# An attention, gated-product and soft-mixture kernel: the gated rows turned by VectorE through DRAM in all batches but the last third of the last, and weight slots opened where the block products end

## The chip, the core and the metric

The kernel runs on one core of a Trainium2 chip. The metric is the device time of one execution in microseconds (us); it is compared as a median of several runs. Engines are named as the profile names them: PE (TensorE, matmuls; PEld its weight loads), DVE (VectorE), ACT (ScalarE), POOL (GpSimd), SP (SyncE, which here only issues transfers).

## What is computed

Four batches of 448 tokens. Attention with a sigmoid in the place of the softmax gives x (1792 x 768); a gated product makes g = (x w_a) * (x w_b), 1536 wide, and x = g w_out; a soft mixture of 8 experts with 32 slots works on that. The reference, cut:

```python
scores = scale * np.matmul(q, k.transpose(0, 1, 3, 2)) - np.log(S)      # S = 448, 12 heads of 64
x = np.matmul(1 / (1 + np.exp(-scores)), v)  # -> (4 * 448, 768)
x = ((x @ w_a) * (x @ w_b)) @ w_out          # 768 -> 1536 -> 768
logits = x @ phi                             # 32 slots
d = softmax(logits, axis=0)                  # over all 1792 tokens
slot_input = (d.T @ x).reshape(8, 4, 768)
for e in range(8):
    slot_out[e] = np.maximum(slot_input[e] @ w1[e], 0) @ w2[e]   # 768 -> 1024 -> 768
out = softmax(logits, axis=1) @ slot_out
```

## The kernel before

All matrices are float32. Weights and x are split into a high and a low part (h, l), so that one product is three matmuls in a fast format.

x is never multiplied by w_out for all tokens. Since d.T @ (g w_out) = (d.T @ g) w_out, the kernel needs G = d.T @ g (32 x 1536) only, and multiplies that by w_out once, at the end. The logits come from g and w_out phi, computed early. G needs g with tokens on partitions, while the products leave it with the 1536 columns on partitions, in 12 chunks (fc) of 128 x 448 per batch. `group(b, gi)` takes four chunks (gi = 0, 1, 2), adds their share of the logits (`project`, L581), and turns them in one of two ways. For gi of 0 and 1, DVE turns 32 x 32 blocks (L603), four SP transfers write them to the DRAM tensor gk32 in runs of 512 bytes (`store_gk`, L641), and two transfers read them back with tokens on partitions in runs of 2 KB (`reload_gk`, L646 and L647). For gi of 2, PE transposes 16 blocks of 128 x 128 (L624), and DVE and ACT copy the four banks out (L626). `LG(b)` makes the logits' exponentials and adds the batch's share of G (`dg`, L936: 48 matmuls, 96 in the trace).

The stages follow each other in one hand-written order per engine. (1) Attention of all batches, with the products of batch 0 (`ab(0)`, L660) in its second quarter. A background job meanwhile rewrites the weights: w_a and w_b to the DRAM tensor ab32, w_out to out32. (2) `unit(u)`, u = 0 to 11: the products of batches 1 and 2 together, as seven block products each (L843). (3) `ab(3)`: the products of batch 3, 72 steps of 6 matmuls. Step i belongs to chunk i // 6; each chunk uses 6 KB per partition of weights, two transfers of 384 KB (`load_w`, L542), numbered LAST + 0 to LAST + 23, that are cast by DVE (L550) and subtracted by POOL (L551). In its first 28 steps the last groups of batches 1 and 2, then LG(1) and LG(2), are mixed in. (4) `last_LG`: logits and G of batch 3. (5) The expert part: G times w_out (L1229), 24 blocks of w1 (1 MB each) in six products of four (L1249), 32 blocks of w2 (768 KB) in eight products of four (L1275), then the output (L1301, L1322, L1323).

The blocks of w_out, w1 and w2 form one queue. `pump()` issues the next one into the next free slot of 8 KB per partition (L1074 for w_out, L1085 for most of w1 and w2, L1080 and L1083 for halves of the last eight blocks of w2). `done(what)` gives a slot back when a product has used it, and pumps again. Slots come from pools that are opened when earlier buffers die: 11 of pool e1 at step 6 of ab(3), two after LG(1), three after LG(2), gkp0 when the last weights no longer use it, e10 after the last weight block, three of e2 when ab(3) is over, the fourth (e20) after G is finished. Before any slot comes back there are thus 22: 5 of w_out and 17 of w1. pump is called every third step of ab(3), from step 12 on.

All transfers but a few stand in SP's one queue, in program order. Each waits for the tiles that it writes to be free, for the data that it reads, and for the eighth transfer before it to have landed, so that at most eight are under way; what stands behind a waiting transfer waits too.

## Time and profile before

| | us |
|---|---|
| median of 3 runs (662.77 to 665.39) | 664.79 |
| the profiled execution | 664.73 |
| its span, first to last instruction | 662.8 |
| PE busy in it | 633.0 (96%) |
| DVE, ACT, POOL busy | 380.1, 296.6, 308.4 |
| HBM read and written | 126.36 MB, 27.17 MB |

The page gives busy times over the span and in 40 slices, the traffic, the costliest groups of instructions, and the chain of work that ended last: from the last instruction back, at each step, to what released it. Other views answer for a stretch: busy time and transfer rate of a window, instructions in order of time, waits, and transfers with their time from issue to landing. A matmul's end is modelled, so a PE that is busy all the time is not PE at its peak.

### The profile page before, as it was taken

The page shows a single profiled execution, that of the slowest core. Times are in us where ns is not written, and L with a number is a line of the kernel's source. Part 1 is how long each engine was busy: PE and PEld are TensorE (multiplying, and loading weights), DVE is VectorE, ACT ScalarE, POOL GpSimd, SP SyncE. Part 2 cuts the span into 40 slices and gives each one's busy share as a digit, 9 for nine tenths or more (in the row PEclk, how much of TensorE's full clock was granted, in tenths as well). Part 3 has the DMA queues.
Part 4 walks back from the last instruction along what each step waited for, and adds up shares of the span by engine and source line. Part 5 has one row for each costly group of instructions (what it writes and reads, how often), then busy time and mean ns, then how long its engine had stood idle before and what let it go on. Part 6 is the DMA issues. An engine that isn't in the chain of part 4 may idle for free.

```text
span 662.8 us, 10904 instructions
## 1 busy us (share of the span) xinstructions
PE 633.0 (96%) x4015; PEld 449.9 (68%) x4015; DVE 380.1 (57%) x557; ACT 296.6 (45%) x534; POOL 308.4 (47%) x236
## 2 busy tenths in 40 slices
PE   6999999999999999999999999999999998997685
PEld 4557777777776555489988989888879895442121
DVE  4765797788774879588777766744324322200013
ACT  4888889889774677754423322202010002110022
POOL 0233676777644248579976575543334441000000
PEclk9999999999999999999999999999999999998798
DMA  9998999989968676501213423242999999999998
GB/s 204 280 258 221 298 305 291 314 268 300 278 166 184 112 150 143 179 1 47 96 49 103 111 89 101 69 134 80 347 372 333 384 369 344 410 415 416 409 374 303
DMA packets 145396, 154.25 MB, mean 233 GB/s; under 512 B 74336, under 2 KB 121792, under 8 KB 142272
## 3 DMA queue, kind: packets, MB, share of 16 engines
q1 hardware_dynamic: 138768, 150.01, 72.5%
q10 hardware_dynamic: 6576, 3.56, 1.9%
q8 instruction: 32, 0.52, 0.3%
q14 instruction: 20, 0.16, 0.1%
HBM read 126.36 MB, written 27.17 MB: 232 GB/s over the span
## 4 chain that ended last, share of the span: by engine, by line
PE 83%; DMA 11%; ACT 2%; DVE 2%; issue 1%; ACTq 1%; SPq 0%; DVEq 0%
PE ab L660 28%; PE sc L843 16%; DMA e<-in_moe_w 9%; PE sc L243 8%; PE ab L843 8%; PE sc L273 5%; PE ab L279 3%; PE ms L195 2%; PE ms L936 2%; PE ms L581 1%; DMA gkp<-in_moe_w 1%; PE ms L480 1%; PE ms L493 1%; PE ab L243 1%; ACT a L249 1%; PE ab L286 1%
## 5 line engine op out<-in xcount | busy, mean ns | idle before, releaser
L454 POOL TENSOR_TENSOR w<-gk,cy 128x768 int32<-128x768 int32 x36 | 66.2, 1842 | 80.1 <-DVE gk L449 35.3
L249 ACT ACTIVATE a<-sc,sums 112x448 f32<-112x448 f32 (+1 forms) x147 | 83.1, 650 | 15.8 <-PE sc L243 15.7
L660 PE MATMUL ab<-t,wh 128*128 128x448 f32 x288 | 65.1, 371 | 0.0
L660 PEld LDWEIGHTS ab<-t,wh 128*128 128x128 f32 x288 | 53.4, 188 | 6.1 <-issue 1.3
L551 POOL TENSOR_TENSOR wl<-wr,wh 128x768 fp32r<-128x768 f32 x16 | 29.5, 1841 | 49.7 <-DVE wh L550 31.9
L551 POOL TENSOR_TENSOR wl<-w,wh 128x768 fp32r<-128x768 f32 x24 | 45.0, 1878 | 10.1 <-ACT wh L550 10.1
L667 ACT COPY misc<-ab 128x448 f32<-128x448 f32 x24 | 12.7, 531 | 82.1 <-PE ab L660 75.2
L1275 PE MATMUL ab<-e,gk 128*32 128x384 f32 x240 | 34.3, 560 | 9.5 <-DMA e<-in_moe_w 9.5
L670 DVE TENSOR_TENSOR misc<-misc,ab 128x448 f32<-128x448 f32 x24 | 14.8, 616 | 43.9 <-PE ab L660 43.9
L273 PE MATMUL sc<-a,vn 112*64 112x448 f32 x192 | 38.7, 545 | 0.2 <-ACT a L249 0.2
L243 PE MATMUL sc<-qh,kh 64*112 64x448 f32 (+1 forms) x147 | 34.9, 447 | 1.0 <-ACT qh L183 0.6
L723 ACT CAST wx<-T 128x384 fp32r<-128x384 f32 x21 | 10.8, 513 | 55.7 <-DVE T L745 39.1
L660 PE MATMUL ab<-xh,wh 128*128 128x448 f32 x144 | 34.9, 377 | 0.0
L660 PE MATMUL ab<-xl,wh 128*128 128x448 f32 x144 | 34.7, 376 | 0.0
L724 POOL TENSOR_TENSOR wx<-T,wx 128x384 fp32r<-128x384 f32 x23 | 24.6, 1070 | 21.1 <-ACT wx L723 18.0
L660 PE MATMUL ab<-xh,wl 128*128 128x448 f32 x144 | 34.3, 373 | 0.0
L660 PE MATMUL ab<-t,wl 128*128 128x448 f32 x144 | 34.3, 373 | 0.0
L724 POOL TENSOR_TENSOR wx<-wr,wx 128x384 fp32r<-128x384 f32 x29 | 32.4, 1117 | 3.7 <-ACT wx L723 3.6
L1322 DVE COPY o<-sc 128x384 f32<-128x384 f32 x10 | 5.4, 554 | 48.2 <-PE sc L1301 47.0
L447 DVE TENSOR_SCALAR mf<-gk 128x768 f32<-128x768 f32 x24 | 22.7, 947 | 17.2 <-ACT gk L430 17.2
L660 PEld LDWEIGHTS ab<-xl,wh 128*128 128x128 f32 x144 | 25.9, 188 | 9.4 <-issue 7.7
L1275 PEld LDWEIGHTS ab<-e,gk 128*32 128x32 f32 x240 | 9.8, 120 | 32.8 <-DMA e<-in_moe_w 20.7
(492 smaller groups left out, 1526.6 us busy)
## 6 DMA issues: line engine op xcount, KB each, us to landing
e<-in_moe_w SPq DMA_DIRECT2D x23, 1024.0 KB, 8.5
e<-in_moe_w SPq DMA_DIRECT2D x23, 768.0 KB, 15.1
wr<-ab SPq DMA_DIRECT2D x14, 768.0 KB, 4.4
ab<-w SPq DMA_DIRECT2D x24, 384.0 KB, 6.4
gk<-gk SPq DMA_DIRECT2D x24, 224.0 KB, 4.0
e<-in_moe_w SPq DMA_DIRECT2D x14, 384.0 KB, 8.8
wr_cv<-in_moe_w_a SPq DMA_DIRECT2D x6, 768.0 KB, 7.9
wr_all<-in_moe_w_b SPq DMA_DIRECT2D x6, 768.0 KB, 6.8
```

What stands on the lines that cost most here:

```text
L243: pe.matmul(sc[h], kx[r, cs], qx[r], start=(i == 0), stop=(i == 2))
L249: act.activation(a, sc, AF.Sigmoid, bias=nlog[:n], scale=1.0 / math.sqrt(D))
L273: pe.matmul(pv[64 * h:64 * h + 64], qkv_t["v", g][:, h, c, :], a_t.pop((g, h, c)), start=(c == 0), stop=(c == C - 1))
L279: pe.matmul(pv[64 * h:64 * h + 64], qkv_t["v", g][:, h, c], a_t.pop((g, h, c)), start=(c == 0), stop=False)
L447: dve.tensor_scalar(mf, m, LOW, HIGH, op0=ALU.max, op1=ALU.min)
L454: pool.tensor_tensor(thirds(w), m.bitcast(I32), thirds(cy_t.pop(x)), op=ALU.add)
L551: pool.tensor_tensor(wl, t, wh.bitcast(F32), op=ALU.subtract)
L660: pe.matmul(t, w[:, kk * 128:(kk + 1) * 128], xt[b * NP + kk][xi], start=(s == 0 and kk == 0), stop=(s == 2 and kk == KD - 1))
L670: dve.tensor_tensor(g, g, t, op=ALU.mult)
L724: pool.tensor_tensor(w[:, 1], t, w[:, 0].bitcast(F32), op=ALU.subtract)
L843: pe.matmul(t, w[:, wi, k * 128:(k + 1) * 128], xs[ORDER[m], k][xi], start=(s == 0 and k == 0), stop=(s == 2 and k == 2))
L1275: pe.matmul(sps[h][32 * j:32 * j + 32], hT[:, 2 * x + i, 2 * j + g], ring[order2[n + j]][0][:, i, c0:c0 + w], start=(g == 0 and x == 0 and ...
```

## The change

- Group 2 of batches 0, 1 and 2 goes the way of groups 0 and 1: DVE turns it, SP stores it, and it is read back. Only group 2 of batch 3 keeps PE's transposes.
- For batches 0 to 2 (TURNED) gk32 gets another layout (t outside n), so that 112 partitions read 8 KB of adjacent bytes each in one transfer, in the place of two transfers with runs of 2 KB. The token order of `weights` and of the exponentials (written with strides) follows from that, and `dg` uses 112 rows in all four parts. Batch 3 keeps the old layout.
- w_out is read as five pieces of a row of 9216 values: four of 8 KB per partition, one of 4 KB; before, three with runs of 2 KB and two with runs of 1 KB. Pieces cut one chunk in two, so that the product has 25 matmuls, not 24.
- Tiles swap places. Of the block products' g, units 0, 1, 6 and 7 use pool xb and units 2, 3, 8 and 9 use gT_all. r0, r1, r2, x3t and the weights' wr move from pool cp to a new pool hp. So xb and cp die with the last unit, and e1 (14 tiles) opens there with eight slots and three tiles each for the reloads of batches 1 and 2; hp dies at step 6, and a pool f1 (3 tiles) takes its place. pump is called from step 0. Batch 3's first chunks wait for the group that still holds their tile (held_by). The groups of batch 1 are now all filed ahead of those of batch 2.
- The number of slots before one comes back: eight of e1, f12, three after LG(1), f11 and three after LG(2), gkp0, f10, four of e2, which is 22.

The diff, cut:

```diff
-NE1, NE2 = 17, 4
+NE1, NF1, NE2 = 14, 3, 4
-    gk32 = drp.tile([B, 2, S, 512], F32, name="gk32")
+    gk32 = [[drp.tile([32, S // 32, 512] if b in TURNED else [S // 32, 32, 512], F32, name=f"gk32_{b}{gi}")
+             for gi in range(3 if b in TURNED else 2)] for b in range(B)]
...
+    def turns(b, gi):
+        return gi < 2 or b in TURNED
...
-        if gi < 2:
+        if turns(b, gi):
             turned = gk[:, :4 * S].rearrange("p (n f) -> p n f", f=128)
...
     def reload_gk(b, gi, t):
+        if b in TURNED:
+            sp.dma_start(out=t[:T], in_=gk32[b][gi].rearrange("t n f -> (t n f)").rearrange("(p x) -> p x", p=T))
+            gtok[b, gi] = t.rearrange("p (c n) -> p c n", c=C)
+            return
...
+    held_by = (None, KF + 8, 2 * KF + 9, 2 * KF + 8, KF + 9)
...
-                            while n - 5 in live or (n % KF == 4 and b and run["lg"] < b - 1):
+                            while n - 5 in live or (n % KF == 4 and b and run["lg"] < b - 1) or (b == B - 1 and held_by[n % 5] in live):
                                 fill_step()
...
         if k < 4:
-            return gT_all[k + 1]
+            return pools["xb"].tile([128, S], F32, tag=f"g{k}", name=f"g{k}")
         if k < 8:
-            return pools["xb"].tile([128, S], F32, tag=f"g{k}", name=f"g{k}")
+            return gT_all[k - 3]
...
-        if b == B - 3:
-            open_slots(run["e1"], [2, 3])
-        elif b == B - 2:
+        if b == B - 2:
             run.pop("lsd2")
-            open_slots(run["e1"], [1, 4, 5])
+            open_slots(run["f1"], [1])
+        if b:
+            open_slots(run["e1"], gtiles[b])
...
+        store_gk(0, 2, turned_0[2])
...
-            i = what[1]
-            if i < 3:
-                t = t.rearrange("p (a n) -> p a n", a=4)
-                src = out32[:, 4 * i:4 * i + 4, :512]
-            else:
-                t = t[:, :6 * 256].rearrange("p (a n) -> p a n", a=6)
-                src = out32[:, 6 * (i - 3):6 * (i - 3) + 6, 512:]
-            sp.dma_start(out=t, in_=src)
+            src = out32.rearrange("p k n -> p (k n)")[:, 2048 * what[1]:min(2048 * what[1] + 2048, KF * DM)]
+            sp.dma_start(out=t[:, :src.shape[1]], in_=src)
...
+    cp_ctx.close()
+    xb_ctx.close()
+    e1 = run["e1"] = ctx.enter_context(tc.tile_pool(name="e1", bufs=1, side="right"))
+    back = [(b, gi) for b in gtiles for gi in range(3)]
...
+    reload_next()
+    reload_next()
+    open_slots(e1, range(6, NE1))
     for i, frac in enumerate(ab(B - 1)):
...
-            open_slots(e1, range(6, NE1))
+            open_slots(f1, [2])
...
-        if i >= 12 and i % 3 == 0:
+        if back and 6 <= i:
+            reload_next()
+        if i % 3 == 0:
             pump()
```

DVE's order from the last unit (L836, L845) into batch 3 before, with L550 the cast of a weight block, L670 the product of a and b:

```order
L836 TENSOR_TENSOR x3t<-x3t,gk_94 128x448
L585 TENSOR_TENSOR misc<-misc,sc 128x448
L626 COPY gk_93<-ms 128x512
L550 CAST wh_4983<-wr 128x768
L626 COPY gk_93<-sc 128x512
L585 TENSOR_TENSOR misc<-misc,ms 128x448
L670 TENSOR_TENSOR misc<-misc,ab 128x448
L626 COPY gk_93<-sc 128x512
L550 CAST wh_5037<-wr 128x768
L626 COPY gk_93<-ms 128x512
```

The same place in the changed kernel (L609 is the turning, L553 the cast, L680 the product, L588 the sum of logits):

```order
L845 TENSOR_TENSOR x3t<-x3t,gk_94 128x448
L588 TENSOR_TENSOR misc<-misc,sc 128x448
L609 STREAM_TRANSPOSE gk_93<-misc 128x14x32 x2
L609 STREAM_TRANSPOSE gk_93<-r_4764 128x14x32
L609 STREAM_TRANSPOSE gk_93<-x3t 128x14x32
L553 CAST wh_4973<-wr 128x768
L588 TENSOR_TENSOR misc<-misc,ms 128x448
L609 STREAM_TRANSPOSE gk_93<-misc 128x14x32 x2
L680 TENSOR_TENSOR misc<-misc,ab 128x448
L609 STREAM_TRANSPOSE gk_93<-r_4811 128x14x32
L609 STREAM_TRANSPOSE gk_93<-r_4794 128x14x32
L553 CAST wh_5013<-wr 128x768
```

Eight turnings stand where four copies of PSUM banks stood, and the two casts keep their places behind them.

SP's queue from the end of the block products before; ab is ab32 (weights), out is out32 (w_out), gk_102 is gk32:

```order
L542 DMA gk_94<-ab_99 128x768 x2
L542 DMA wr<-ab_99 128x768 x2
L646 DMA e_5063<-gk_102 128x3x512
L647 DMA e_5063<-gk_102 64x512
...
L542 DMA gk_94<-ab_99 128x768
L1074 DMA e_5141<-out_100 128x4x512
L542 DMA gk_94<-ab_99 128x768
L1074 DMA e_5174<-out_100 128x4x512
```

The same place in the changed kernel (L545 is load_w, L645 the stores, L649 a reload, L1083 w_out; gk_12_107 is batch 1, group 2):

```order
L545 DMA gk_94<-ab_99 128x768 x2
L649 DMA e_4937<-gk_10_105 112x2048
L649 DMA e_4939<-gk_11_106 112x2048
L1083 DMA e_4948<-out_100 128x2048
L645 DMA gk_12_107<-gk_93 448x1x128 x4
L1083 DMA e_4988<-out_100 128x2048
L645 DMA gk_22_110<-gk_93 448x1x128 x4
L545 DMA wr<-ab_99 128x768 x2
L649 DMA e_5036<-gk_12_107 112x2048
L1083 DMA e_5038<-out_100 128x2048
...
L1083 DMA e_5076<-out_100 128x2048
L545 DMA gk_94<-ab_99 128x768
```

Two reloads and two pieces of w_out moved ahead of the weights LAST + 6 and LAST + 7 (wr), eight stores came in between, and four reloads and two pieces of w_out stand ahead of LAST + 8 (the last row).

SP's queue over the last third of ab(3) in the changed kernel; L1094 is a block of w1, L654 and L655 the reloads of batch 3, the last row but one is e20:

```order
L1094 DMA e_5554<-in_moe_w 128x2048
L1094 DMA gkp_5580<-in_moe_w 128x2048
L545 DMA wr<-ab_99 128x768 x4
L654 DMA gk_93<-gk_30_111 128x3x512
L655 DMA gk_93<-gk_30_111 64x512
L654 DMA gk_93<-gk_31_112 128x3x512
L655 DMA gk_93<-gk_31_112 64x512
L1094 DMA f_5741<-in_moe_w 128x2048
L1094 DMA e_5789<-in_moe_w 128x2048
L1094 DMA e_5791<-in_moe_w 128x2048
L1094 DMA e_5793<-in_moe_w 128x2048
L1094 DMA e_5899<-in_moe_w 128x2048
```

Before, blocks of w1 stood between the last four weight loads (wr); now they are all ahead of them, and gkp, the last of them, is pumped at step 48.

## Rows read from the trace of the kernel before

**Rows 1.** The page, busy tenths in 40 slices of the span:

```profile
PE   6999999999999999999999999999999998997685
PEclk9999999999999999999999999999999999998798
DMA  9998999989968676501213423242999999999998
```

**Rows 2.** The chain that ended last, 545 us on: start, length, engine and line:

```profile
550.42 0.88 PE ms L581 x6
...
556.36 3.48 PE ab L936 x96
...
561.64 4.08 PE sc L1229 x48
...
569.54 3.69 PE sc L1249 x32
573.24 0.22 SPq L1085
573.54 10.98 DMA e<-in_moe_w
...
630.16 8.36 DMA gkp<-in_moe_w
638.56 1.49 PE ab L1275 x10
```

**Rows 3.** Windows: length, busy time per engine, PE clock, DMA share, GB/s:

```profile
440.00:460.00 20.00, 20.00 (x119) 16.39 (x118) 9.73 (x17) 2.88 (x5) 5.58 (x4) 1.00 0.09 23
460.00:500.00 40.00, 40.00 (x361) 32.20 (x361) 14.20 (x32) 4.94 (x13) 13.74 (x8) 1.00 1.02 353
573.00:647.00 74.00, 61.03 (x453) 21.44 (x449) 5.77 (x11) 6.22 (x13) 0.00 (x0) 0.93 1.03 404
```

**Rows 4.** SP's instructions in order of time, 455 us on: start, length, line:

```profile
458.48 0.80 SPq L542 DMA_DIRECT2D wr<-ab  x2
...
547.27 12.95 SPq L1085 DMA_DIRECT2D e<-in_moe_w  x5
561.38 0.59 SPq L1218 DMA_DIRECT2D misc<-clog  x1
562.77 24.02 SPq L1085 DMA_DIRECT2D e<-in_moe_w  x16
```

**Rows 5.** Line 1085, the three blocks issued when ab(3) ends, and their landing:

```profile
L1085 SPq DMA_DIRECT2D e<-in_moe_w x3: 346/431/432, 550.4 to 551.3; - x3
...
DMA to landing us min/median/max: 6.0/8.0/10.0
```

**Rows 6.** The chain by line over 441 to 476 us, and its piece at chunk 4:

```profile
by line: PE ab L660 64.4%; PE ms L936 9.8%; PE sc L843 6.4%; PE ms L624 5.9%; PE sc L624 5.0%; PE sc L581 2.5%; PE ms L581 2.5%; PE ms L881 2.1%; PE sc L925 1.0%; PE sc L919 0.9%
...
485.01 1.41 PE ab L660 x6
```

**Rows 7.** Line 603, turnings on DVE: shortest, median, longest in ns, first and last start:

```profile
L603 DVE STREAM_TRANSPOSE gk<-r x3: 630/633/636, 396.5 to 416.2; 128x448 f32<-128x448 f32 x3
```

**Rows 8.** The chain that ended last, 210 to 220 us:

```profile
211.88 1.45 DVE kl L184
...
217.43 1.02 PE ms L624 x8
...
219.25 0.59 PE ms L624 x4
```

**Rows 9.** SP in order of time, one k load (four transfers) of attention:

```profile
254.94 2.09 SPq L153 DMA_DIRECT2D kn<-in_k  x4
```

**Rows 10.** DVE in order of time, the first use of that load:

```profile
265.52 0.63 DVE L191 STREAM_TRANSPOSE kn<-kn 128x448 f32<-128x448 f32 x1
```

**Rows 11.** Line 641, SP's stores of batches 1 and 2:

```profile
L641 SPq DMA_DIRECT2D gk<-gk x16: 303/650/1256, 355.2 to 430.1; - x16
...
DMA to landing us min/median/max: 2.7/4.0/5.5
```

**Rows 12.** Line 646, the 2 KB part of the reloads of batches 1 and 2:

```profile
L646 SPq DMA_DIRECT2D e<-gk x4: 587/638/1581, 459.3 to 463.9; - x4
...
DMA to landing us min/median/max: 6.8/8.4/11.0
```

**Rows 13.** Line 542, the weights LAST + 6 and LAST + 7:

```profile
L542 SPq DMA_DIRECT2D wr<-ab x2: 320/372/424, 458.5 to 458.9; - x2
...
DMA to landing us min/median/max: 4.0/4.3/4.6
```

**Rows 14.** Line 542, the weights LAST + 5:

```profile
L542 SPq DMA_DIRECT2D gk<-ab x1: 333/333/333, 444.6 to 444.6; - x1
...
DMA to landing us min/median/max: 3.0/3.0/3.0
```

**Rows 15.** Line 550, casts of weight blocks on DVE:

```profile
L550 DVE CAST wh<-wr x6: 518/552/560, 449.3 to 498.5; 128x768 fp32r<-128x768 f32 x6
```

More of the change, by code (lines that the diff above doesn't have):

```diff
@@ L46, in body @@
     stat = ctx.enter_context(tc.tile_pool(name="stat", bufs=2, side="left"))
-    ps_ctx, ab_ctx, x0_ctx, cv_ctx, at_ctx, cp_ctx, xb_ctx = (ctx.enter_context(ExitStack()) for _ in range(7))
+    ps_ctx, ab_ctx, x0_ctx, cv_ctx, at_ctx, hp_ctx, cp_ctx, xb_ctx = (ctx.enter_context(ExitStack()) for _ in range(8))
     lgp = ctx.enter_context(tc.tile_pool(name="lgp", bufs=1, side="left"))
@@ L300, in raw_x @@
         nm = f"r{kk}" if b == 2 else "x3t"
-        return pools["cp"].tile([128, S], F32, tag=nm, name=nm)
+        return pools["hp"].tile([128, S], F32, tag=nm, name=nm)
     def emit_x(g):
@@ L535, in body @@
     LAST = 2 * (NCH - KF)
+    gtiles = {1: (0, 1, 2), 2: (3, 4, 5)}
     def load_w(x):
@@ L604, in group @@
                 yield
-                if b < B - 1:
+                if b < B - 1 and gi < 2:
                     yield
@@ L618, in group @@
         gk = gk.rearrange("p (c n) -> p c n", c=C)
-        if gi == 2 and not b:
-            yield
         for c in range(C):
@@ L692, in ab @@
                         run.pop("wr")
-                        open_slots(run["e1"], [0])
+                        open_slots(run["f1"], [0])
                         pump()
@@ L864, in unit @@
         if u % 4 == 3:
+            fill.append(group(1, u // 4))
             fill.append(group(2, u // 4))
-            fill.append(group(1, u // 4))
     def col():
@@ L920, in tokens, with weights @@
         dve.tensor_copy(dst, t)
-    def weights(d, dst):
+    def weights(b, d, dst):
         t = ms((128, C, NS))
+        if b in TURNED:
+            for c in range(C):
+                pe.transpose(t[:T, c], d[:NS, c::C], ident[:NS, :NS])
+            dve.tensor_copy(dst[:T], t[:T])
+            return
         for c in range(C):
@@ L956, in rest_LG @@
     def rest_LG(b, dtok):
-        weights(run["lsd"][1], dtok)
+        weights(b, run["lsd"][1], dtok)
         for _ in range((3, 4, 1)[b]):
@@ L960, in rest_LG @@
         gp = ms((128, FF // 4))
-        for groups in ((0,), (1,), (2,)):
-            dg(b, dtok, gp, groups)
+        for gi in range(3):
+            dg(b, dtok, gp, gi)
         if b:
@@ L995, in last_LG @@
         dtok = wphi[:, 4:4 + C]
-        weights(run["lsd"][1], dtok)
+        weights(B - 1, run["lsd"][1], dtok)
         for _ in gr:
@@ L1000, in last_LG @@
         gp = ms((128, FF // 4))
-        for groups in ((0,), (1,), (2,)):
-            dg(B - 1, dtok, gp, groups)
+        for gi in range(3):
+            dg(B - 1, dtok, gp, gi)
         dve.scalar_tensor_tensor(acc, acc, run["al"], gp, op0=ALU.mult, op1=ALU.add)
@@ L1176, in body, with reload_next @@
     load_w(LAST + 5)
+    cp_ctx.close()
+    xb_ctx.close()
+    e1 = run["e1"] = ctx.enter_context(tc.tile_pool(name="e1", bufs=1, side="right"))
+    back = [(b, gi) for b in gtiles for gi in range(3)]
+    def reload_next():
+        b, gi = back.pop(0)
+        nm = f"e1{gtiles[b][gi]}"
+        reload_gk(b, gi, e1.tile([128, 2048], F32, tag=nm, name=nm))
+    reload_next()
+    reload_next()
+    open_slots(e1, range(6, NE1))
     for i, frac in enumerate(ab(B - 1)):
@@ L1183, in body @@
                 fill_step()
-            cp_ctx.close()
-            xb_ctx.close()
-            e1 = run["e1"] = ctx.enter_context(tc.tile_pool(name="e1", bufs=1, side="right"))
-            run["lsd2"] = e1.tile([128, 2048], F32, tag="e11", name="lsd2")
-            run["wr"] = e1.tile([128, 2048], F32, tag="e10", name="wr")
+            hp_ctx.close()
+            f1 = run["f1"] = ctx.enter_context(tc.tile_pool(name="f1", bufs=1, side="right"))
+            run["lsd2"] = f1.tile([128, 2048], F32, tag="f11", name="lsd2")
+            run["wr"] = f1.tile([128, 2048], F32, tag="f10", name="wr")
             load_w(LAST + 6)
             load_w(LAST + 7)
-            for x in range(4):
-                nm = f"e1{2 + x}"
-                reload_gk(1 + x // 2, x % 2, e1.tile([128, 2048], F32, tag=nm, name=nm))
-            open_slots(e1, range(6, NE1))
+            open_slots(f1, [2])
             fill.append(LG(1))
@@ L1223, in body @@
     for what in order0:
-        i = what[1]
-        h, n, f0 = (0, 4, 4 * i) if i < 3 else (1, 6, 6 * (i - 3))
-        for x in range(n):
-            fc = f0 + x
-            j = fc % 4
-            pe.matmul(sip[h][32 * j:32 * j + 32, :512 - 256 * h], GT[:, fc * NS:(fc + 1) * NS], ring[what][0][:, x],
-                      start=(fc < 4), stop=(fc >= 8))
+        lo, hi = 2048 * what[1], min(2048 * what[1] + 2048, KF * DM)
+        cuts = [c for fc in range(KF) for c in (fc * DM, fc * DM + 512) if lo < c < hi]
+        for a, z in zip([lo] + cuts, cuts + [hi]):
+            fc, n0 = divmod(a, DM)
+            h, j = n0 // 512, fc % 4
+            n0 -= 512 * h
+            pe.matmul(sip[h][32 * j:32 * j + 32, n0:n0 + z - a], GT[:, fc * NS:(fc + 1) * NS],
+                      ring[what][0][:, a - lo:z - lo], start=(fc < 4), stop=(fc >= 8))
         done(what)
```

36 lines of the change are left out of this document (19 added, 17 removed).

## The prediction

> **What bounds the kernel now.** I read the page's slices first, then the chain of waits, then the same stretch by windows and by SP's instructions in order of time.
>
> The slices [rows 1] show two regimes. PE is at nine tenths in every slice but the first up to the expert part, at a granted clock of nine tenths or more. The DMA line is low in the third quarter (the block products of batches 1 and 2), full again from about slice 28, and full to the end. The chain [rows 2] tells which of them ends last where both are high. Up to the product of G by w_out (L1229, at 561.64) it is PE pieces; behind the first w1 product (L1249, at 569.54) it is a row of transfers, the first of them issued at 573.24 and the last block (gkp) landing at 638.5, then the short output. So the kernel is bound by PE up to about 562 and by DMA after it.
>
> The joint between the two is what decides. A tail transfer can only go out when a slot comes back, and the first slot comes back when L1229 has used a block of w_out: SP issues five blocks at 547.27 and after, then the next run of blocks at 562.77 [rows 4]. From there on the transfer share is 1.03 at 404 GB/s over 74 us, with PE busy 61 of them [rows 3]. Before that release 22 blocks are in, whatever SP did earlier. Both kernels have 22 slots. Hence what moves the end is **when the PE path reaches L1229**; it shifts the whole DMA tail with it. How early the 22 blocks were loaded only matters if they would otherwise be late.
>
> I make the sum against the profiled execution: 664.73 us, its span 662.8, so 1.9 lies around the span. The median of the runs is 664.79, so no correction is needed.
>
> **Part (b): groups 2 of batches 1 and 2 leave PE.** They stand in the first third of ab(3): 32 transposes of 128 x 128. In the chain between 441 and 476 the two forms of L624 hold 5.9% and 5.0% of 35 us [rows 6]: 10.9% of 35 = 3.8 us. PE was busy 20.00 of 20.00 us there [rows 3], so nothing else ends last and the time comes off in full: **-3.8**. DVE gets eight turnings of 0.63 each [rows 7], 5.0 us, in the place of four copies of PSUM banks. It was busy 9.73 of 20 us there [rows 3], so it has room; two weight casts stand behind turnings, and PE needs the first at step 6, some 8 us after the stage begins (six steps of 1.41 [rows 6]). Cost nothing; if that cover were gone it would be up to four turnings, 2.5.
>
> **Part (a): group 2 of batch 0.** It lies in attention, with 16 transposes. Eight and four of them are on the chain, 1.02 and 0.59 [rows 8]; the other four run while DVE's chain ends last there (kl, L184, in the same rows). That is -1.61. Against it, DVE now has a turning of 0.63 more ahead of its own k work, on the same chain: net **-1.0**. SP gets four more stores, about 2.09 / 4 = 0.52 each in issue [rows 9], 2.1 in all, ahead of a k load. That load was issued from 254.94 to 257.0 and first used by DVE at 265.52 [rows 9, 10]; a landing of some 3 us leaves over 5 us to spare, so 2.1 is hidden. Bounds: -1.6 with DVE's turning hidden, +1.1 with SP's 2.1 us and DVE's 0.63 both on the path (-1.6 + 0.6 + 2.1).
>
> **The new term: a weight block that comes late in ab(3).** The removed time was PE's, but transfers were added in front of the weights. In the order of SP's queue six reloads, four blocks of w_out, two groups of stores and the weights LAST + 6 and + 7 now stand ahead of LAST + 8, which chunk 4 needs at step 24. Before, the transfer share in 440 to 460 was 0.09 [rows 3] and the queue began at 458.48 [rows 4], so this is a dense pack that starts when LAST + 5, issued at 444.6, has landed 3.0 later [rows 14]: 447.6.
>
> - Bytes: 6 x 0.918 + 4 x 1.049 + 3 x 0.393 = 10.9 MB. The rate for runs of 8 KB: three blocks issued 0.45 us apart landed 6.0, 8.0 and 10.0 us after issue [rows 5], so 1.049 MB per 2.45 us, 428 GB/s: 25.4 us.
> - Stores: two groups of four, under way together. One store took 4.0 from issue to landing, 2.7 to 5.5 [rows 11]. Two times 4.0 is 8.0.
> - 447.6 + 25.4 + 8.0 = 481.0, and the cast of it 0.55 [rows 15]: 481.6.
> - PE begins chunk 4 at 485.01 before [rows 6], less 3.8 = 481.2. The stall is **+0.4**.
>
> The bounds of this term: if DMA queues hide the stores under each other (2.7 a group), no stall, 0. If the pack runs at the 353 GB/s of 460 to 500 before [rows 3], where runs were 512 bytes to 8 KB, 10.9 MB take 30.9, and with stores of 5.5 the block lands at 489.5; the stall is then 8.9. The reloads of before, runs of 2 KB, took 6.8 to 11.0 to land [rows 12], but four of them were issued within 4.6 us and waited for one another. I take a value near the low end because all but the stores and weights now are in rows of 8 KB, as in rows 5. Chunk 3 is safe: LAST + 6 and + 7, which landed 4.0 to 4.6 after issue before [rows 13], have 4.7 MB and two store groups ahead of them, 447.6 + 11.0 + 8.0 = 466.6; PE comes to chunk 3 six steps of 1.41 ahead of chunk 4, or earlier by what is mixed in: with the 96 matmuls of one dg (3.5 [rows 2]) at 481.2 - 8.5 - 3.5 = 469.2, still after the cast.
>
> **Small edits, at nothing.** The product with w_out has 25 matmuls instead of 24 and a scaling at its end (some 0.25 of PE), covered by the tail's DMA: four slots' transfers are already under way then. Exponentials with strides, chunks that wait for a group's tile (held_by): PE has steps of other work to fill. w_out in runs of 8 KB and in less DMA time: before the release, so hidden. Without the cover, together about 0.5.
>
> [...] By rows 6 the transposes cost 3.8 us of an engine that is never idle there, and DVE is free for half of the time. [...]
>
> **Sum:** 664.7 - 1.0 - 3.8 + 0.4 = **660.3**.
>
> **Rivals.**
>
> *Rival 1, the gain is eaten: 664.5.* Part (a) comes out at its bad bound (+1.1 instead of -1.0) or DVE's chains of turnings delay casts by up to 2.5, and the stall at chunk 4 is near 2: 664.7 - 3.8 + 1.1 + 2.0 + 0.5 = 664.5. For it: SP's single queue, in which the new stores hold all that follows; the margin at chunk 4 is nearly zero in my own sum. Against: each place had 5 us of cover in rows 3, 9 and 10. [...]
>
> *Rival 2, the prefetch pays: 651.2.* Transfers start at about 445 instead of 458.48 [rows 4]; if the DMA stream is one whole from there to the end, its end moves by 13.5 us: 664.7 - 13.5 = 651.2. For it: the DMA line of the page is full from there on [rows 1], and a share of 0.09 in 440 to 460 is room. Against: 22 slots are full long before the release, SP then stands still (before, for most of 12.95 us at 547.27 [rows 4]; now from the last pump at step 48, some 25 us more), and the tail starts at the release all the same.
> [...]
>
> *Rival 3, slower: weights starve.* One mechanism, LAST + 8 late behind the reloads and stores, at the other bound above: landing 489.5, cast 490.1, against a PE that is there at 481.2: stall 8.9. 664.7 - 1.0 - 3.8 + 8.9 = 668.8. It decides when LAST + 8 lands later than 485.4, where stall and gain (4.8) are equal. For it: in 460 to 500 the share was already 1.02 with 353 GB/s [rows 3]. Against: much of that traffic was in short runs, which this change removes.
>
> **How the numbers follow.** The change gives PE's time back and little else: 0.62, at 660.3. Rival 1: 0.22. Rival 2: 0.06. Rival 3: 0.10. My own case spans 657.5 (both gains whole, -1.6 and -3.8, no stall, and up to 2 us from a smoother ab(3)) to some 663.5. The range reaches over most of rival 1 above: 657.5 to 665.5, leaving out rivals 2 and 3 and a little more. About 0.5% (3.3 us) is what a measurement of this kernel can tell from no change; faster than 661.4 is some four fifths of my case and rival 2, 0.50 + 0.06 = 0.56. Slower than 668.1 is rival 3: 0.10. The rest, 0.34, is no difference.
>
> **What would show it.** Right: PE transposes only for batch 3; ab(3)'s end some 4.5 us earlier than 550.4; L1229's successor at about 557 instead of 561.64 and SP's next block about 1 us behind it; the last block landing near 642 in a row of transfers at 400 GB/s or more; a DMA line that falls for about 25 us before the end of ab(3). Wrong: a PE idle for several us before step 24, waiting for a cast (rival 3 and, smaller, rival 1); attention that ends as late as before or later (part (a)); a first release at 558 but a tail that is shorter than before by more than 2 us (rival 2); a tail that is longer, by a way that I don't see.

## The result, and the profile after

The changed kernel takes 672.97 us (median of 5 runs, 668.8 to 675.1), the kernel before 664.79. The ratio is 1.0117, with a 95% interval of 1.0077 to 1.0157. So it is slower by 1.2%, 8.2 us; the forecast was 660.3, in a range of 657.5 to 665.5. The way in which it is slower is near that of rival 3, which the prediction gave 1 chance in 10: PE stands for late transfers, but at two places, not at one.

The page of the changed kernel, busy tenths in 40 slices, to be held beside [rows 1]:

```profile
PE   6999999999999999999999999999769998997685
PEclk9999999999999999999999999999869999999899
DMA  9999999999877677703124414559999978999998
```

PE, which had nine tenths in every slice of this part, shows a 7 and a 6 in slices 29 and 30, with the granted clock down in the same place, and DMA has filled the gap ahead of it. Windows of that place (length, busy time of PE, PEld, DVE, ACT, POOL, granted clock, DMA share, GB/s), after:

```profile
440.00:460.00 20.00, 20.00 (x105) 15.77 (x104) 12.44 (x25) 2.51 (x6) 6.82 (x5) 1.00 0.91 278
460.00:470.00 10.00, 6.77 (x88) 5.86 (x87) 0.71 (x2) 0.53 (x1) 2.73 (x2) 1.00 0.90 258
470.00:480.00 10.00, 9.40 (x64) 8.17 (x65) 2.71 (x7) 0.93 (x2) 1.83 (x1) 0.83 1.03 297
480.00:490.00 10.00, 3.89 (x23) 2.99 (x21) 0.76 (x3) 1.03 (x4) 0.07 (x1) 0.76 1.01 333
490.00:500.00 10.00, 10.00 (x119) 8.63 (x120) 3.83 (x8) 0.54 (x1) 4.16 (x3) 0.73 1.03 414
```

Between 440 and 460 the transfers moved 23 GB/s before and 278 now [rows 3]. From 460 to 490 PE lacks 3.23 + 0.60 + 6.11 = 9.9 us. And look at the last number of each row: the DMA engines are fully busy (share 0.9 to 1.03), but move only 258 to 333 GB/s, while 414 are reached a moment later. What PE waited for (us in total, times, longest), 455 to 500, after:

```profile
PE ab L670 <- DVE wh L553: 6.1, 1, 6.1
PE ms L950 <- DMA e<-gk: 3.8, 1, 3.8
```

Two waits. The short one comes first: LG(1)'s dg (L950) has done 64 of its 96 matmuls and stands for the third reload of batch 1 (e<-gk). The long one is chunk 4, which stands for the cast of LAST + 8. PE's instructions in order of time around them (start, length; in brackets the idle time before and what ended it), after:

```profile
464.82 1.96 PE L950 MATMUL ms<-e,lsd 112*32 112x128 f32 x64
470.60 1.08 PE L950 MATMUL ms<-e,lsd 112*32 112x128 f32 x32 [3.82 <-DMA e<-gk]
471.61 2.61 PE L670 MATMUL ab<-t,wl 128*128 128x448 f32 x6
...
489.86 2.61 PE L670 MATMUL ab<-t,wh 128*128 128x448 f32 x6 [6.11 <-DVE wh L553]
492.40 4.30 PE L950 MATMUL ms<-e,lsd 112*32 112x128 f32 x96
```

After each wait six matmuls of a step take 2.61 us, where a step took 1.41 before [rows 6]. A window of the second such stretch (columns as above):

```profile
490.00:492.00 2.00, 2.00 (x6) 1.68 (x6) 1.40 (x4) 0.00 (x0) 1.76 (x1) 0.50 0.97 399
```

The granted clock is 0.50 there, half of the 1.00 that the windows from 440 to 470 have. Further windows show 0.50 up to 495 here, and 0.50 to 0.51 from 471.7 to 475, behind the first wait. Then SP, in order of time, after:

```profile
454.41 5.03 SPq L645 DMA_DIRECT2D gk<-gk  x4
459.57 4.62 SPq L545 DMA_DIRECT2D wr<-ab  x2
464.23 0.43 SPq L649 DMA_DIRECT2D e<-gk  x1
...
467.55 0.38 SPq L545 DMA_DIRECT2D gk<-ab  x1
```

One row of what SP stood for between 455 and 500 (us in total, times, longest), after:

```profile
SPq L545 <- DMA clog<-lsd: 3.7, 1, 3.7
```

And the chain that ended last over that stretch (start, length, engine and line), after:

```profile
458.43 5.42 DMA clog<-lsd
...
463.86 0.32 SPq L545
...
467.55 21.58 DMA gk<-ab
...
489.24 0.57 DVE wh L553
...
489.86 2.61 PE ab L670 x6
```

Two things ended late in a row. The second of LAST + 6 and + 7 (L545 wr) was issued 4.3 us after the first, when ACT's small transfer of LG(1)'s logits (clog) had landed. Only three other transfers were under way at that moment, so SP stood for clog itself, by its place in the order, and not for room among the eight. And LAST + 8, issued at 467.55, landed 21.6 us later, at 489.1.

From there on the kernel runs as the old one did, but later. SP's blocks around the first release in order of time, after:

```profile
556.25 9.78 SPq L1094 DMA_DIRECT2D e<-in_moe_w  x4
...
569.01 3.41 SPq L1094 DMA_DIRECT2D e<-in_moe_w  x5
```

The window of the tail (columns as in the windows above), after:

```profile
573.00:647.00 74.00, 60.20 (x450) 23.28 (x450) 5.86 (x10) 4.58 (x8) 0.00 (x0) 0.98 1.02 408
```

The product with w_out starts at 567.45 (561.64 before), the first release is at 569.01 (562.77), and the tail runs at 408 GB/s (404 [rows 3]). The span is 668.5, 5.7 longer. The profiled execution itself took 673.0, so 4.5 us lie around its span, 1.9 before; that part the trace doesn't explain. The spans of the five runs are 666.7 to 672.9, and the time around them is 4.0 and 4.5 us in two of them, 2.1 to 2.2 in the other three. So of the 8.3 us between the two profiled executions the traces account for 5.7.

### The profile page after: what moved, and what is told of

Read it like the earlier page. It is cut to its first block, busy times and chain, and to the rows that moved or that the text cites. A ratio compares the mean times of both kernels' runs of the same rounds, so it can differ in the third digit from the quotient of the medians.

```text
span 668.5 us, 10815 instructions
## 1 busy us (share of the span) xinstructions
PE 626.2 (94%) x3969; PEld 450.3 (67%) x3969; DVE 382.4 (57%) x561; ACT 295.4 (44%) x530; POOL 310.0 (46%) x236
## 4 chain that ended last, share of the span: by engine, by line
PE 79%; DMA 12%; DVE 3%; ACT 2%; SPq 1%; issue 1%; ACTq 0%; DVEq 0%
PE ab L670 25%; PE sc L852 16%; PE ab L852 7%; PE sc L245 6%; PE sc L275 5%; DMA gk<-ab 3%; PE sc L1272 3%; PE ab L281 2%; DMA f<-in_moe_w 2%; DMA e<-in_moe_w 2%; PE ms L197 2%; PE ms L584 1%; DMA gkp<-in_moe_w 1%; PE ms L482 1%; PE ms L950 1%
## 5 line engine op out<-in xcount | busy, mean ns | idle before, releaser
L251 ACT ACTIVATE a<-sc,sums 112x448 f32<-112x448 f32 (+1 forms) x147 | 82.8, 647 | 13.6 <-PE sc L245 13.5
L670 PE MATMUL ab<-t,wh 128*128 128x448 f32 x288 | 65.4, 375 | 6.1 <-DVE wh L553 6.1
L670 PEld LDWEIGHTS ab<-t,wh 128*128 128x128 f32 x288 | 55.0, 193 | 12.0 <-DVE wh L553 6.2
L677 ACT COPY misc<-ab 128x448 f32<-128x448 f32 x24 | 12.7, 529 | 112.8 <-PE ab L670 106.1
L554 POOL TENSOR_TENSOR wl<-w,wh 128x768 fp32r<-128x768 f32 x24 | 46.4, 1937 | 9.4 <-ACT wh L553 9.4
L680 DVE TENSOR_TENSOR misc<-misc,ab 128x448 f32<-128x448 f32 x24 | 14.8, 615 | 43.6 <-PE ab L670 43.6
L1298 PE MATMUL ab<-e,gk 128*32 128x384 f32 x200 | 31.0, 528 | 9.0 <-DMA e<-in_moe_w 9.0
L670 PE MATMUL ab<-t,wl 128*128 128x448 f32 x144 | 35.1, 380 | 0.0
L670 PE MATMUL ab<-xh,wh 128*128 128x448 f32 x144 | 34.9, 377 | 0.0
L670 PE MATMUL ab<-xl,wh 128*128 128x448 f32 x144 | 34.7, 376 | 0.0
L734 POOL TENSOR_TENSOR wx<-T,wx 128x384 fp32r<-128x384 f32 x23 | 25.0, 1085 | 20.8 <-ACT wx L733 17.7
L670 PE MATMUL ab<-xh,wl 128*128 128x448 f32 x144 | 34.3, 373 | 0.0
L670 PEld LDWEIGHTS ab<-xl,wh 128*128 128x128 f32 x144 | 25.9, 188 | 9.4 <-issue 7.7
L245 PEld LDWEIGHTS sc<-qh,kh 64*112 64x112 f32 (+1 forms) x147 | 16.4, 200 | 21.2 <-issue 12.5
```

The source lines that it names most:

```text
L245: pe.matmul(sc[h], kx[r, cs], qx[r], start=(i == 0), stop=(i == 2))
L251: act.activation(a, sc, AF.Sigmoid, bias=nlog[:n], scale=1.0 / math.sqrt(D))
L554: pool.tensor_tensor(wl, t, wh.bitcast(F32), op=ALU.subtract)
L670: pe.matmul(t, w[:, kk * 128:(kk + 1) * 128], xt[b * NP + kk][xi], start=(s == 0 and kk == 0), stop=(s == 2 and kk == KD - 1))
L680: dve.tensor_tensor(g, g, t, op=ALU.mult)
L734: pool.tensor_tensor(w[:, 1], t, w[:, 0].bitcast(F32), op=ALU.subtract)
```

## What was run

Ratios are to the kernel before in runs on the same chip. "Idle" is PE's time without work between the first and the last product of batch 3 in the profiled execution.

| kernel | us | ratio (95%) | idle, us |
|---|---|---|---|
| as changed | 672.97 | 1.0117 (1.0077 to 1.0157) | 9.9 |
| clog_late | 673.02 | 1.0132 (1.0112 to 1.0152) | 9.8 |
| rows128 | 665.23 | 1.0010 (0.9994 to 1.0025) | 4.1 |
| rows128pad | 668.14 | 1.0050 (1.0032 to 1.0067) | 5.1 |
| rows128pad_pump6 | 669.62 | 1.0076 (1.0047 to 1.0104) | 7.1 |
| rows128pad_pump9 | 668.56 | 1.0054 (1.0037 to 1.0071) | 6.5 |
| rows128pad_clog_late | 668.52 | 1.0069 (1.0052 to 1.0086) | 5.7 |
| rows128pad_pump6_clog_late | 670.16 | 1.0088 (1.0064 to 1.0111) | 7.6 |
| rows128pad_pump9_clog_late | 667.86 | 1.0059 (1.0038 to 1.0080) | 7.0 |
| rows128pad_clog_sp | 664.75 | 1.0001 (0.9982 to 1.0020) | 4.8 |
| rows128pad_pump9_clog_sp | 663.97 | 0.9988 (0.9975 to 1.0001) | 2.3 |
| pump12 | 667.79 | 1.0052 (1.0032 to 1.0073) | 4.9 |
| chunks112_pump12 | 667.94 | 1.0053 (1.0034 to 1.0072) | 6.1 |
| runs2k_pump12 | 667.56 | 1.0055 (1.0028 to 1.0082) | 3.9 |
| pe_turns_all | 661.99 | 0.9970 (0.9957 to 0.9983) | 0 |
| pe_turns_b12 | 662.35 | 0.9963 (0.9946 to 0.9980) | 0 |
| rows128pad_b2_pe_clog_sp | 660.69 | 0.9938 (0.9923 to 0.9953) | 0 |

### Is it part (b)'s transfers? Group 2 back on PE

```diff
 def turns(b, gi):
-    return gi < 2 or b in TURNED
+    return gi < 2 or b == 0          # pe_turns_all: gi < 2
...
-back = [(b, gi) for b in gtiles for gi in range(3)]
+back = [(b, gi) for b in gtiles for gi in range(2)]
```

> Edit: group 2 of batches 1 and 2 is turned by PE again, so eight stores and two of the six reloads are gone, pump from step 0 stays. (The token order of that group no longer fits the weights, so the output is off; every instruction's size stays.) Theory A: the pack is shorter by two store groups (8 us) and two reloads (3.7 each), LAST + 8 lands near 474, no idle time in ab(3); the transposes are back on PE (3.8); the time is 664.8 less attention's gain of 3, so 661 to 663. Rival B gives about the same here. Rival C (the early w_out blocks alone are enough to starve PE): idle time of 5 us or more stays, 666 or more.

> Edit: as pe_turns_b12 (662.35), and group 2 of batch 0 is turned by PE too: part (a) is undone, with its four stores and its reload; no stall stands in either. (Token order of the groups turned by PE doesn't fit the weights.) By the prediction's own step part (a) is worth 1.0 us: 663.4. If the earlier start of batch 3's stage in the changed kernel (439.8 for 442.9) were all part (a), 665.4.

Measured 662.35 and 661.99, ratios 0.9963 and 0.9970, with no idle time in batch 3's stage in either. Without part (b), everything else of the change (slots from the end of the block products, pump from step 0, w_out in 8 KB rows, the new layout) is harmless, and together it gains 0.3%; the loss comes when the eight stores and two reloads of part (b) are added. Part (a) is worth 0.07% (0.5 us) between these two, with intervals of 0.13 to 0.17% on either side: neither zero nor the 1.0 us of the prediction is excluded.

### How fast is a reload?

> Not the kernel: six loads back to back of each of eight forms, alone on the chip, output zero. In order: (a) 112 rows of 8 KB from a DRAM tile that the kernel wrote in runs of 512 bytes, (b) 128 rows of 8 KB from w1, (c) 112 rows of 8 KB from w1, (d) 128 rows of 7 KB from the tile, (e) runs of 2 KB in two transfers (384 and 64 runs) from the tile, (f) 128 rows of 8 KB at a stride of 36 KB, (g) 96 rows of 8 KB from w1, (h) 64 and 48 rows of 8 KB from the tile, then (a) and (b) again. Theory A2: (a), (c) and perhaps (g), (h) take 3 to 3.7 us per 0.92 MB, the packets of 8 KB 420 to 530 ns; (b), (d), (e), (f) run at 2.2 to 2.5 with packets of 8 KB at 310 ns. Rival D, source: (a), (d), (e), (h) are slow, (c) is as quick as (b). Rival D, mix: all forms take 310 ns per 8 KB when alone.

Windows from the first landing of a form to a late one, in the order (a) to (h); the columns are length, DVE, POOL, granted clock, DMA share and GB/s:

```profile
66.83:80.97 14.14, 0.00 (x0) 0.00 (x0) 1.00 1.01 259
88.92:98.94 10.02, 0.00 (x0) 0.00 (x0) 1.00 1.01 428
108.17:123.49 15.32, 0.00 (x0) 0.00 (x0) 1.00 1.01 259
131.21:139.96 8.75, 0.00 (x0) 0.00 (x0) 1.00 1.01 424
147.83:158.21 10.38, 0.00 (x0) 0.00 (x0) 1.00 1.06 348
165.41:175.37 9.96, 0.00 (x0) 0.00 (x0) 1.00 1.01 429
184.38:198.89 14.51, 0.00 (x0) 0.00 (x0) 1.00 1.01 223
206.43:230.34 23.91, 0.00 (x0) 0.00 (x0) 1.00 1.02 194
```

The first and third rows are the changed kernel's reload, 112 rows of 8 KB: four of them in 14.14 and 15.32 us, 3.5 to 3.8 each, 259 GB/s in both windows, from the scratch tile and from w1 alike. Form (a), run again at the end, took 3.1 each (293 GB/s), so it varies, but stays slow. The same bytes as 128 rows of 7 KB (fourth row) go at 424 GB/s, four in 8.75. The form before, two transfers in runs of 2 KB (fifth), takes 2.6 each. So the source doesn't explain it, and the new form made the reload slower, not faster.

> Not the kernel: again six loads back to back of each form, alone on the chip, output zero. (a) 112 partitions, each four runs of 2 KB, from the DRAM tile; (b) 112 partitions, each two runs of 4 KB; (c) 112 rows of 8 KB to partitions 16 to 127; (d) 128 rows of 7 KB; (e) 112 rows of 2 KB from w1; (f) 128 rows of 2 KB from w1; (g) 120 rows of 8 KB from w1; (h) 64 rows of 8 KB from w1. Theory E (a transfer to fewer than 128 partitions is slow, whatever the runs): (a), (b), (c) take 3 us or more for 0.92 MB, (d) 2.2. Theory F (few long runs per transfer are slow, partitions don't matter): (a) takes 2.6 as the two transfers of 2 KB runs did, (c) 3.5, (b) between them. If it were the first partition, (c) would differ from 3.5.

The windows of (a), (b), (c), (d), (g) and (h):

```profile
67.36:83.44 16.08, 0.00 (x0) 0.00 (x0) 1.00 1.06 229
91.88:104.00 12.12, 0.00 (x0) 0.00 (x0) 1.00 1.03 302
112.82:124.63 11.81, 0.00 (x0) 0.00 (x0) 1.00 1.01 312
132.18:141.03 8.85, 0.00 (x0) 0.00 (x0) 1.00 1.01 425
165.35:183.69 18.34, 0.00 (x0) 0.00 (x0) 1.00 0.95 214
193.70:203.95 10.25, 0.00 (x0) 0.00 (x0) 1.00 1.01 205
```

This is theory E: every form with fewer than 128 partitions is slow. 112 partitions are slow with runs of 2 KB (4.0 us each), 4 KB (3.0) and 8 KB; 120 are no better (214 GB/s), 64 get 205; 128 get 425. All the time the DMA share is near 1: the engines look busy. The partitions are not all that counts, as the spread among the forms of 112 shows, 229 to 312 GB/s. The two forms of 0.2 MB in runs of 2 KB, (e) and (f), lie closer together in windows of their own: 222 GB/s to 112 partitions, 299 to 128. Why fewer partitions are slow these loads don't show.

Then in the kernel:

```diff
-sp.dma_start(out=t[:T], in_=....rearrange("(p x) -> p x", p=T))        # T = 112
+sp.dma_start(out=t[:, :1792], in_=....rearrange("(p x) -> p x", p=128))   # rows128
```

> Edit: the six reloads of batches 1 and 2 read the same bytes as 128 rows of 7 KB in the place of 112 rows of 8 KB. (Tokens then land on other partitions, so the output is off; the work on all engines stays.) Theory A2 (112 rows are what makes a reload take 3.7 us where a block of 1 MB takes 2.45): a reload takes 2.2, the pack is 9 us shorter, LAST + 8 lands near 480, idle in ab(3) 1 to 3 us, time 661 to 665. Rival D (reading what was just written, or the mix with other transfers, is slow): reloads stay at 3.5 or more and the time at 671 to 674.

Measured 665.23, a ratio of 1.0010: of the 1.2% lost this one size is about nine tenths, and of the 12.7 us between forecast and measurement somewhat more than half. LAST + 8 was issued at nearly the same time, 467.3, and landed after 15.3 us, not 21.6 (line 545 in rows128, with its landing):

```profile
L545 SPq DMA_DIRECT2D gk<-ab x1: 385/385/385, 467.3 to 467.3; - x1
...
DMA to landing us min/median/max: 15.3/15.3/15.3
```

That is 482.6, 6.5 us earlier. The gain isn't whole: PE still waits twice, 1.6 and 2.5.

```diff
-gk32 tile [32, 14, 512]; t[:112] <- 112 rows
+gkw tile [128, 2048], gk32 its first 112 rows; t <- 128 rows     # rows128pad, batches 1 and 2
```

> Edit: in DRAM each group of batches 1 and 2 gets 16 rows of padding, and the reload reads 128 rows of 8 KB, 16 of which nobody uses (1.049 MB in the place of 0.918); tokens and all else as changed, pump from step 0. The padding is written once, during the block products. Theory A2: a transfer of 128 rows takes 2.47 us where 112 rows took 3.5 to 3.9, although it moves more; LAST + 8 lands near 484, idle in ab(3) 4 to 6 us, time 664 to 667, as rows128 (665.2). If the 112 rows were not the cause: 672.

668.14: better than 673 with a transfer that moves 14% more, and worse than rows128, whose six reloads have 0.8 MB less. Reloads queued behind each other land 2.5 us apart here, 3.7 in the changed kernel, and where that one moved 297 GB/s a window of rows128pad shows, at the same DMA share:

```profile
470.00:480.00 10.00, 8.89 (x61) 7.71 (x62) 2.71 (x7) 0.40 (x1) 1.83 (x1) 0.83 1.01 426
```

### Fewer blocks ahead of the weights

```diff
-if i % 3 == 0:
+if i >= 12 and i % 3 == 0:        # pump12; 6 and 9 in _pump6, _pump9
     pump()
```

> Edit: blocks of w_out and w1 are pumped from step 12 of ab(3) on, as before the change, not from step 0; all else as changed. Theory A (the loss is the weight blocks LAST + 6 to LAST + 8 landing late behind a dense pack of transfers): four blocks of w_out leave the pack ahead of LAST + 8, 10 us or more; it lands at 476 to 480 in place of 489, PE's idle time in ab(3) falls from 9.9 us to under 3, and the time to 660 to 664. Rival B (the waits come from the chain of turnings on DVE and the stores on SP, not from the amount of data): the idle time stays near 10 us, the time near 672.

> Edit: pump from step 12 as in pump12, and the reloads of batches 0 to 2 read 112 partitions in four runs of 2 KB each, tokens in chunks of 112 in natural order, in the place of one run of 8 KB. Theory F: a reload takes 2.6 us in the place of 3.7, LAST + 8 lands near 475, no idle time in ab(3), dg keeps its 2.76 us; the time is 664.6 - 1.0 (part a) - 3.8 (part b) - 2.1 (three dg of 2.76 for 3.44) + 0.5 (25 matmuls of w_out) = 658.2. Theory E: reloads stay at 3.5, the result is near that of pump12, 667.

> Edit: pump from step 12, and the layout of gk32, reloads and token order as before the change (two transfers with runs of 2 KB, 128 partitions). Both theories: a reload takes 2.6 to 2.9, LAST + 8 lands near 476, idle in ab(3) under 1.5; dg is back at 3.44. 664.6 - 1.0 - 3.8 + 0.5 = 660.3, up to 663 if the weights' last loads wait for blocks of w1 as in pump12 (a gap of 2.2 us at 538).

> Edit: rows128pad, and pump from step 9 on, so that one block of w_out instead of four stands ahead of LAST + 8 and none ahead of LAST + 6. Theory A (late weights are the whole loss): LAST + 8 lands near 477, no idle time before step 24; 664.4 less 3.8 (transposes of batches 1 and 2), 2.1 (three dg of 2.76 for 3.44) and 0.3 (part a), plus 0.5 (w_out product): 658.7. Rival G (the blocks pumped later collide with the last weight loads, as in pump12 and runs2k_pump12, with gaps at 531 to 540): 662 to 666.

> Edit: rows128pad, and pump from step 6 on: two blocks of w_out ahead of LAST + 8, none ahead of LAST + 6. Theory A: LAST + 8 lands near 479.5, idle 0 to 1 us, 659 to 660. Rival G: the late collision is one pump further off than with step 9, so 659 to 663.

All five took 667.6 to 669.6. For runs2k_pump12, rows128pad_pump9 and rows128pad_pump6 that is slower than any theory had said (658.7 to 666); pump12 lies between its two (660 to 664, 672); chunks112_pump12, at 667.9, came as theory E said (667), by which 112 partitions are slow in runs of 2 KB too (229 GB/s in micro2). Two other waits took the place of the one removed. The first stands in SP's waits of rows128pad_pump9, 440 to 500:

```profile
SPq L1097 <- DMA clog<-lsd: 8.9, 1, 8.9
SPq L652 <- DMA clog<-lsd: 7.9, 1, 7.9
```

SP stood at a reload for 7.9 us, until ACT's 56 KB of LG(1)'s logits had landed, and at a block for those of LG(2). The second is late in the stage; SP in order of time in pump12:

```profile
526.16 0.33 SPq L545 DMA_DIRECT2D wr<-ab  x1
534.00 0.33 SPq L1094 DMA_DIRECT2D e<-in_moe_w  x1
534.42 0.38 SPq L545 DMA_DIRECT2D wr<-ab  x1
```

SP issues nothing from 526.5 to 534.0. One row of what it stood for, 500 to 545:

```profile
SPq L1094 <- DMA gk<-gk: 7.5, 1, 7.5
```

These are ACT's stores of batch 3's groups, which take up to 9.2 us to land here, and the next weight block stands behind the block that waits. PE then waits 2.2 us at 538.5. Blocks that weren't pumped in the first twelve steps have to go out here. The kernels with pump from step 0 have no gap here, so the early pump costs near step 24 of ab(3) and pays near step 60.

### The stand for ACT's transfer

```diff
-(act if b else sp).dma_start(out=clog32[:, :, b], in_=ltok[:T])
+if b == 1: run["clog"] = lambda: act.dma_start(out=clog32[:, :, 1], in_=ltok[:T])   # called at i == 14
+else: ...
```

> Edit: the changed kernel, only that ACT's transfer of LG(1)'s logits to DRAM (clog) is issued at step 14 of ab(3), behind LAST + 8 and LAST + 9 in program order, not at once. Theory H (SP's wait for clog's landing, 458.4 to 463.9, is a part of the loss by itself): the reload of batch 1's group 2 is issued near 460 in place of 464.2 and lands 1 to 3 us earlier than 470.6, the first gap (3.8) halves; LAST + 8 stays near 487, since the queue behind it is full anyway; 670 to 672. Theory A2 alone (rate): nothing changes, 673.

> Edit: rows128pad (reloads of 128 rows, pump from step 0) with clog at step 14. Theory H: without the stand of 5.1 us at LAST + 7 the reload lands by 467, no first gap; LAST + 8 near 481.5, second gap about 2; 662 to 665 in place of 668. If the wait for clog costs nothing: 668.

> Edit: rows128pad_pump6 with clog at step 14. Theory H: SP doesn't stand 7.6 us at a block of w_out; LAST + 8 lands near 478, no gap before step 24. Left is the wait for ACT's stores at 534 (a gap of 2 at 539): 660 to 663 in place of 669.6. If clog costs nothing: 669.

> Edit: rows128pad_pump9 with clog at step 14. Theory H: SP doesn't stand 7.9 us at a reload; LAST + 8 lands near 475, no gap before step 24. Left are gaps of 1 to 3 us at 531 to 540: 660 to 664 in place of 668.6. If clog costs nothing: 668.

Nothing changed (673.0, 668.5, 670.2, 667.9), and this told nothing of theory H, because the edit moved the stand and didn't remove it. SP in rows128pad_clog_late:

```profile
459.64 2.39 SPq L547 DMA_DIRECT2D wr<-ab  x2
467.17 0.32 SPq L652 DMA_DIRECT2D e<-gk  x1
```

ACT issued clog at 463.8, later by its own order, and SP, which runs ahead of it, stood for its landing at the reload instead, until 467.2. The edit that removes it lets SP issue the transfer, behind LAST + 8:

```diff
-(act if b else sp).dma_start(out=clog32[:, :, b], in_=ltok[:T])
+(act if b == 2 else sp).dma_start(out=clog32[:, :, b], in_=ltok[:T])
```

> Edit: rows128pad (reloads of 128 rows, pump from step 0), and LG(1)'s clog is issued by SP, where it stands behind LAST + 8, in the place of ACT. Theory H: SP no longer stands near 459; the reload of batch 1's group 2 is issued near 460 and lands by 468, so the first gap falls from 2.8 to about 1; LAST + 8 near 482.5 and a second gap of 1 to 2: 664 to 666 in place of 668. If the queue is full anyway: 668.

> Edit: rows128pad_pump9 with LG(1)'s clog issued by SP behind LAST + 8. Theory H: LAST + 8 lands near 475.5 in place of 481.4, the gap of 3 us at 479 is gone. Left are the gaps of 1 to 2 us at 533 and 539, where SP stands for ACT's stores: 663 to 666 in place of 668.6. If the stand at clog cost nothing: 668.

664.75 and 663.97, 3.4 and 4.6 us less than the same kernels without this edit, as theory H said of the times. SP in rows128pad_clog_sp:

```profile
459.05 2.21 SPq L547 DMA_DIRECT2D wr<-ab  x2
461.31 0.43 SPq L652 DMA_DIRECT2D e<-gk  x1
...
466.11 0.57 SPq L966 DMA_DIRECT2D clog<-lsd  x1
```

The reload is issued at 461.3, not 465.6 as in rows128pad. The mechanism is whole in rows128pad_pump9_clog_sp alone: the gap of 3.2 us at 479 is gone, no idle time is left before 500, and its 2.3 us are all near 529 and 536. In rows128pad_clog_sp the first gap falls from 2.8 to 1.4, but the second grows from 2.3 to 3.3, where 1 to 2 was expected. The idle time is nearly the same, 4.8 for 5.1, and the stage of batch 3 is 2.0 us shorter; so the rest of its 3.4 us is not explained by this wait.

### A faster version, with one group's token order left out

```diff
+ rows128pad_clog_sp, and
-    return gi < 2 or b in TURNED
+    return gi < 2 or b in (0, 1)
```

> Edit: rows128pad_clog_sp, with group 2 of batch 2 turned by PE again: one reload and four stores fewer. (Its token order doesn't fit the weights.) Theory A: LAST + 8 lands near 478, no gap in ab(3); pe_turns_b12 was 0.9963 of before, 662.3; one batch's 16 transposes are off PE, 1.9: 660.5. If any weight still comes late, 663 or more.

660.69, a ratio of 0.9938 (0.9923 to 0.9953), 0.2 from what was expected, and faster than both kernels. It shows a time, not a finished kernel: it leaves out the token order of batch 2's group 2, and what that would cost was not measured. Two of its windows over the stretch in which the changed kernel stood:

```profile
460.00:470.00 10.00, 10.00 (x76) 8.48 (x78) 2.71 (x6) 0.78 (x2) 4.22 (x3) 1.00 1.02 416
...
480.00:490.00 10.00, 10.00 (x134) 8.55 (x133) 3.84 (x8) 0.53 (x1) 3.90 (x3) 1.00 0.94 375
```

PE is busy throughout at a granted clock of 1.00, and about the same DMA share moves 416 and 375 GB/s, not 258 and 333.

## Why the prediction was wrong, point by point

**What held.** PE's path to the product with w_out sets the end: that product came 5.8 us later, and the span grew by 5.7. The product itself takes 4.58 us for 4.08, but from its start to the end of the span it is 101.1 for 101.2: the tail covers it, as the prediction said of the small edits. Rival 2, the prefetch that pays in full, is refuted. In pe_turns_all the slots open and fill as early as in the changed kernel; the time falls by 2.2 us, not 13.5. Of the 3.8 us for part (b)'s 32 transposes one half was tested and bears it out: with those of one batch gone (rows128pad_b2_pe_clog_sp against pe_turns_b12, both without idle time) the stage from the first to the last product of batch 3 is 1.6 us shorter, 104.8 for 106.5, where half of 3.8 is 1.9. That all 3.8 can be had was not shown, since no kernel with both batches turned by DVE was free of idle time.

**The step that failed is the new term**, the +0.4: PE stood 6.1 us for LAST + 8, and 3.8 for a reload ahead of it. All the term's bytes went by one rate, 428 GB/s from rows 5, and the value near its low end was taken "because all but the stores and weights now are in rows of 8 KB". Rows 5 are transfers to 128 partitions; the reloads go to 112, at 259 GB/s alone. Six of 0.918 MB then take 6 x 3.54 = 21.2 us in the place of 12.9. Nothing in the trace of before had 112 partitions in a transfer of this size, and the prediction treated the length of a run as the only thing that sets a rate.

With this one number the sum says 481.0 + 8.4 = 489.4 for LAST + 8, which landed at 489.1. That it is so close, and close to the high bound of 489.5 too (which was made of short runs), is luck. The pack did not start at 447.6: SP doesn't wait for LAST + 5 to land, the first reload was issued at 441.9 (rival 2 itself reckoned with 445), and the pack took 47.2 us, where the sum had 33.4. In rows128, with the reloads to 128 partitions (424 GB/s alone), it took 39.9 (442.7 to 482.6); so 7.3 of the 13.8 us are the reloads' rate. The other 6.5 were not taken apart. In them stores landed 7.2 to 9.4 us after issue, not 4.0; SP stood 3.0 us for DVE's turnings, which ended at 446.2, and 3.7 for clog; and six transfers that SP issued behind LAST + 8, from 468.0 to 488.2, were under way before it landed.

**A consumer was left out.** The term looked at LAST + 8, and at LAST + 6 and + 7, which came near the time forecast (465.7 and 467.4; 466.6 was said), by the same luck of an early start and a longer pack. But the reload of batch 1's third group stands behind them, and dg needs it before chunk 4 does: 3.8 of the 9.9 us.

**A wait across queues was left out.** SP's transfer waits for one that ACT issued. That each transfer waits for the eighth before it was in the description of the queue (neither trace, before or after, has more than eight under way), and the old trace had such a wait too (4.1 us for clog), but there SP stood behind LAST + 8, not ahead of it. Without it the kernels with 128 rows take 3.4 and 4.6 us less; that the wait is the whole of it is shown for the second alone. The changed kernel with this one edit was not run.

**What a wait costs beyond itself.** The stage of batch 3 grew from 107.5 to 116.4 us, by 8.9: -3.8 for the transposes as forecast, -1.4 for two dg that got shorter (below), +9.9 idle, which makes 4.7. The other 4.2 (3.6, if the transposes are put at twice the 1.6 measured) are in stretches at the lower clock: two steps of 2.61 us for 1.41, one of 1.84 and a dg of 4.30 for 2.8 are together some 4.3 longer. Ahead of the stage the profiled execution gained 3.1 us (it begins at 439.8, not 442.9), where the sum had 1.0. Rival 3 had one stall of 8.9 where two came, 9.9 together; without the lower clock, and without the 2.6 us more around the span, it said 668.8. The middle rows of the table have such stretches too: over 480 to 490 the granted clock is 0.66 in rows128 and in pump12, and 1.00 in pe_turns_b12, which has no idle time. How much of the gain the lower clock cancels in these rows, no run separates.

**Part (a)** was put at -1.0 and stays open: 0.5 us by the medians, with zero and 1.0 inside the intervals. Of the 3.1 us that the stage begins earlier, 0.7 are LG(0)'s shorter dg; the start differs from execution to execution (439.8 to 441.2 in the changed kernel, clog_late, pump12, pe_turns_b12 and rows128, which are the same up to there; 441.7 in pe_turns_all), so the rest can't be put down to part (a).

**DVE's turnings and the length of a run.** No wait of PE in batch 3's stage ended at DVE's turnings: one ended at a reload (3.8 us), one at the cast of LAST + 8 (6.1). The reloads were late, and with one batch fewer the move pays (0.9938 in rows128pad_b2_pe_clog_sp). A longer run does help where only the run changes: to 112 partitions, runs of 2 KB took 4.0 us, runs of 4 KB 3.0, runs of 8 KB 3.0 to 3.8. That misled the term here, because the partitions changed with the run: 3.5 us in runs of 8 KB to 112 partitions, 2.6 in runs of 2 KB to 128 and 64.

**What stays open.** Why 112 partitions are slow. Why 4.5 us lie around the changed kernel's span in its profiled execution and 1.9 before. How the 6.5 us of the longer pack that the reloads' rate leaves divide. And whether the stage has room for both batches' transfers: rows128pad_pump9_clog_sp comes within 2.3 us of idle time, all of it behind SP's stand of 8.7 us for ACT's stores of batch 3, and moving those was not tried.
